# A GELU layer and its gradients on one core: new order of q's rests, one units' slot moved, w1's gradient's rests first, first stores behind a load

## The chip, the core and the metric

The kernel runs on one core of a Trainium2 chip. A core has a matrix engine (TensorE, in the profile PE, its weight loads PEld), VectorE (DVE), ScalarE (ACT), GpSimd (POOL) and SyncE (SP), which here only issues transfers. Each engine works through its own instruction stream in order, and engines wait for one another through semaphores. Matmuls read on-chip memory and write PSUM, eight banks of 512 float32 columns on 128 rows of partitions; VectorE and ScalarE empty those banks. The metric is the device time of one execution in microseconds (us); lower is better.

## The reference: what is computed

A layer with x of 2048 rows and D = 448 columns, a hidden width of F = 1792, in bfloat16, and the gradients of all its inputs for a given grad_out g:

```python
def _fwd_reference(x, w1, b1, w2, b2):
    h = jnp.einsum("bsd,df->bsf", x, w1) + b1
    h = _gelu(h)
    return jnp.einsum("bsf,fd->bsd", h, w2) + b2
...
    _out, _vjp = jax.vjp(_f, x, w1, b1, w2, b2)
    _grads = _vjp(grad_out)
```

So there are six large products: u = x w1, h = gelu(u + b1), out = h w2 + b2; q = g w2 transposed, gh = q times the derivative of gelu at u, the gradient of x = gh w1 transposed; then the gradient of w1 = x transposed times gh, and that of w2 = h transposed times g. The gradients of b1 and b2 are sums of gh and g over the rows.

## The kernel before

**Tiling.** The rows are worked in 4 blocks of 512 columns (`SB`), the hidden width in 14 tiles of 128, two tiles to a step: 28 steps numbered k (or f where u is meant; f runs two steps ahead). u and q of a step are two PSUM banks each, with 512 columns. The contraction over D = 448 is three full tiles of 128 and a rest of 64.

**Row halves.** From the third step on almost every matmul of the first two phases is a half product: it uses 64 of the array's 128 rows, the low or the high ones (`half_product`, L259; the matmul is L265). Half products are emitted in pairs, one low, one high, into two different banks (`side_by_side`, L308), and run beside each other. A bank that was written from one half and is next written from the other needs a turn: L260 to L264 put an empty PE instruction ahead that waits for the last matmul of the old half, unless PE has waited for a later one already. The rests of 64 rows lie in one half only (`u_tail`, `q_tail`): in blocks 0 and 1 u's rest is low and q's high, in blocks 2 and 3 the other way round, so that rests of u and q run beside each other.

**Units.** A unit is 128 rows of out (kind o) or of the gradient of x (kind x): one bank, 14 tiles of contraction in h or gh. Two units are open together and are worked as pairs of half products (`units_side`); `second` True is the other half of the contraction. Units' pairs are put between the groups of u and q to give banks time to turn or to be emptied. A finished unit is evicted (`evict`, L437): VectorE adds b2 for kind o, ScalarE copies for kind x, into one of five staging tiles, and POOL's queue stores it.

**Single steps** (L556 to L622, k = 1 to 11). A step emits u's first group (three pairs), units, u's second group with the banks exchanged between the halves, units, the rests of u and q, units, q's first group, units, q's second group, units; `between` lists the units' pairs of these places. ScalarE copies u out of its banks (`copy_u`, L345), then squares, gelu and tanh; VectorE makes the derivative and the product gh (`dve_gh`, L403), which frees q's banks. In the single steps u's banks are the same two each time.

**Double steps** (L646 to L696, k = 12, 14, ... 26). Two steps at once, the odd k and the even k. `pe_tails` (L284) emits u's rests for the next pair interleaved with q's rests for this one; `pe_q_rows` then emits the groups of q, the odd k first. q of the even k has PSUM tile two0. q of the odd k has PSUM tile two1, which in between holds the two units of the step (`open_two(1, 2)`, L675). These are evicted in the next step inside `dve_gate` (L365), from k = 16 on behind its second scalar addition.

**The last phase.** x and g are loaded once more with rows on partitions, gh has been turned by transposing transfers (`turn_gh`) and h was stored and comes back transposed. The gradient of w1 is made in `gw1_full` (L778; 16 matmuls of 128x128 for each of three tiles of D and four groups of columns) and, for the 64 rest columns of x, in `gw1_tail` (L788): pairs of 128x64 matmuls side by side in the array's column halves. Then come the 14 tiles of w2's gradient (`gw2_tile`, L809). Sums for the biases run on VectorE and POOL beside it.

**Queues.** The order on each engine is the order of emission, written out by hand. SP issues nearly all loads, all transposing transfers and the stores of h; POOL the stores of units and a few copies; ACT the stores of the weights' gradients. `behind` (L125) puts an empty instruction on an engine that waits for a transfer.

Of the kernel before, what the change touches and what calls it, by code (L numbers as in the profile page):

```python
# [19 lines left out]
def kernel(  # L20
# [15 lines left out]
    nc = tc.nc  # L36
    P = 128
# [10 lines left out]
    NPAIR = NF // 2  # L48
    NSTEP = NB * NPAIR
    NSINGLE = 12  # L50
# [4 lines left out]
    WIDE = (0, 1)  # L55
# [27 lines left out]
    w1T_sb = const.tile([P, NF, D], BF16, name="w1T_sb")  # L83
# [41 lines left out]
    def behind(eng, transfer):  # L125
        tc.add_manual_dep(eng.nop().ins, transfer.ins.name, mybir.DependencyInfo(mybir.DependencyClass.Sync, mybir.DependencyReason.DATA),
                          reason="loads behind what is needed first")
# [49 lines left out]
    nc.gpsimd.dma_start(out=b2_bc[:], in_=b2.rearrange("(o d) -> o d", o=1).to_broadcast((P, D)))  # L177
    load_w2T(0, 256)
    def load_w1T(t0, t1):
        nc.sync.dma_start_transpose(out=w1T_sb[:, t0:t1, :], in_=w1[:, t0 * P:t1 * P])  # L180

    load_w1T(2, 8)
    load_w1T(8, 12)
    load_g(1)
    load_w1T(12, NF)
    load_w1T(0, 2)

    pw = two_banks(1, "pw")
    for w in range(NWAKE):
# [57 lines left out]
    def half(up):  # L247
        return slice(DL, P) if up else slice(0, DL)

    def open_q(k):  # L250
        b, p = divmod(k, NPAIR)
        if p == 0:
            ghT[b] = blk.tile([P, NF, SB], BF16, name="ghT", tag="ghT")
        PQ[k] = two_banks(0 if k < NSINGLE else order_b[k % 2], "pq")

    LOW, HIGH = slice(0, DL), slice(DL, P)
# [17 lines left out]
    def q_tail(k, a, swap=False):  # L274
        b, p = divmod(k, NPAIR)
        hf = half((b in WIDE) != swap)
        g = g_swap[b] if swap else gT[b][:, 0, :]
        half_product(("q", k, a), PQ[k][:, a, :], w2T[hf, 0, cols(p, a)], g[hf, :], hf, True, False)
# [5 lines left out]
    def pe_tails(fs, ks):  # L284
        cross = bool(fs) and bool(ks) and (fs[0] // NPAIR in WIDE) != (ks[0] // NPAIR in WIDE)
        for k in ks:
            open_q(k)
        us = [(f, a) for f in fs for a in range(2)]
        qs = [(k, a) for k in ks for a in range(2)]
        if not us and len(ks) == 2:  # L290
            for a in range(2):
                q_tail(ks[0], a)
                q_tail(ks[1], a, swap=True)
            return
        for n in range(max(len(us), len(qs))):
            if n < len(us):
                u_tail(*us[n])
            if n < len(qs):
                q_tail(*qs[n], swap=cross)
# [28 lines left out]
    def units_side(uns, second, tiles=range(NF)):  # L328
        one, other = uns[::-1] if second else uns
        side_by_side(unit_of(one, tiles), unit_of(other, tiles))  # L330
        for un in uns:
            un.slots += len(tiles)
        if one.slots == 2 * NF:
            for un in uns:
                un.done = NPAIR
                open_units.remove(un)
                finished.append(un)
# [139 lines left out]
    def evictions(most=NS):  # L477
        for un in finished[:most]:
            un.evict()
        del finished[:most]  # L480
# [42 lines left out]
    uns = [open_units[0:2], open_units[2:4]]  # L523
# [6 lines left out]
    def two_units(banks):  # L530
        for n in banks:
            open_unit(one_bank(n, "ps")[:, 0:D])
        return open_units[-2:]

    def fill(part):
        if isinstance(part, tuple):
            part = [(part[0], part[1], t) for t in part[2]]
        for uns, second, t in part:
            units_side(uns, second, [t])

    def tiles(p):
        return range(2 * p, 2 * p + 2)
# [12 lines left out]
    act_gelu([2])  # L555
    for i in range(1, NSINGLE):  # L556
        f = i + LEAD
        if i < 6:
            between = [(uns[1], False, tiles(i)), (uns[0], True, tiles(i)[:1]), (uns[0], True, tiles(i)[1:]), (uns[1], True, tiles(i))]
        elif i == 6:  # L560
            between = [(uns[0], True, tiles(i)), (uns[1], False, tiles(i)[:1]), (uns[1], False, tiles(i)[1:]), (uns[1], True, tiles(i))]
        else:
            if i == 7:
                ahead, later = xs, two_units((2, 3))
                slots = [(ahead, False, t) for t in range(6, NF - 2)] + [(later, False, t) for t in range(4)]
                slots += [(ahead, False, t) for t in range(NF - 2, NF)] + [(later, False, t) for t in range(4, NF)]
                slots += [(ahead, True, t) for t in range(NPAIR)] + [(later, True, t) for t in range(NF)]
                slots += [(ahead, True, t) for t in range(NPAIR, NF)]
            between = [slots[2 * c:2 * c + 2] for c in range(5)]
            del slots[0:10]  # L570
        open_u(f)
        open_q(i)
        if i == 1:
            fill(between[0])
        side_by_side(u_of(f, 0, True), u_of(f, 1, True))
        if i > 1:
            fill(between[0])
        else:
            fill(between[1])
        side_by_side(u_of(f, 1), u_of(f, 0))  # L580
        if i > 1:
            fill(between[1])
        pe_tail_pair(f, i, 1)
        pe_tail_pair(f, i, 0)
        fill(between[2])
        side_by_side(q_of(i, 0), q_of(i, 1))
        fill(between[3])
        side_by_side(q_of(i, 1, True), q_of(i, 0, True))
        if i < 6:
            units_side(uns[0], False, tiles(i + 1))  # L590
        elif i > 6:
            fill(between[4])
        if i > 1:
            act_tanh([i])
        if i == 6:
            evictions(2)
        copy_u(f, "aa")
        if i == NSINGLE - 1:
            evictions(2)
        act_square([f])  # L600
        if i == NSINGLE - 1:
            evictions()
        act_gelu([f])
        if i == 1:
            dve_chain("both 1", "cubic 2", "gate 1", "cubic*u 2", "slope 2", "gh 1", "slope*h 2", "cubic 3")
        elif i < NSINGLE - 1:
            dve_chain(f"both {i}", f"cubic*u {i + 1}", f"gate {i}", f"slope {i + 1}", f"gh {i}", f"slope*h {i + 1}", f"cubic {f}")
        else:
            dve_chain(f"both {i}", f"cubic*u {i + 1}", f"gate {i}", f"slope {i + 1}", f"slope*h {i + 1}", f"gh {i}",
                      f"cubic {f}", f"cubic*u {f}", f"slope {f}", f"slope*h {f}")  # L610
        if i == 6:
            evictions()
            open_two(1, 2)
            xs = open_units[-2:]
            units_side(xs, False, range(0, 6))
        if i == 9:
            nc.gpsimd.dma_start(out=g_low[0:DL, :], in_=gT[1][DL:P, 0, :])
            g_swap[1] = g_low
        if i < 8 or i % 2:
            traffic(i if i < 8 else (i + 7) // 2)  # L620
        if i > 6:
            stores(2, f - 1)  # L622
# [23 lines left out]
    for n in range(nq):  # L646
        i = 10 + n
        k = NSINGLE + 2 * n
        ks = [k, k + 1]
# [22 lines left out]
        if nxt:  # L672
# [3 lines left out]
            uns = open_units[-2:]  # L676
# [5 lines left out]
        elif fs:  # L682
            uns, held = two_units(order_a[2:4]), two_units(order_a[0:2])
# [17 lines left out]
    for banks in (order_a[2:4], None, order_a[0:2], order_a[2:4]):  # L701
        if banks is None:
            open_two(0, 2)
            uns = open_units[-2:]
        else:
            uns = two_units(banks)
# [81 lines left out]
    def gw1_tail(ft0, n):  # L788
        ps = bank_w()
        for st_ in range(NS):  # L790
            b, j = PLACE[st_]
            for h in range(2):
                nc.tensor.matmul(ps[h * DL:(h + 1) * DL, 0:n * P], lhsT=x_nat[:, st_, KF * P:D],  # L793
                                 rhs=gh_nat[:, b, ft0 + h * n:ft0 + (h + 1) * n, j, :], start=(st_ == 0), stop=(st_ == NS - 1),
                                 tile_position=(0, h * DL), skip_group_check=True)
        o = stg.tile([P, SB], BF16, name="st", tag="st")
        nc.scalar.copy(out=o[:, 0:n * P], in_=ps[:, 0:n * P])
        for h in range(2):
            t0, t1 = ft0 + h * n, ft0 + (h + 1) * n
            while t0 < t1:  # L800
                t2 = t0 + 1
                while t2 < t1 and f_at(t2) == f_at(t2 - 1) + P:
                    t2 += 1
                c0 = (t0 - ft0 - h * n) * P
                queued.append(nc.scalar.dma_start(out=out_2[KF * P:D, f_at(t0):f_at(t0) + (t2 - t0) * P],
                                                  in_=o[h * DL:(h + 1) * DL, c0:c0 + (t2 - t0) * P]))
                t0 = t2

    def gw2_tile(ft, halves):  # L809
# [8 lines left out]
            queued.append(nc.scalar.dma_start(out=out_4[ft * P:(ft + 1) * P, h * w:(h + 1) * w], in_=o[:, 0:w]))  # L818
        return done

    for ft0, n in ((0, 4), (4, 4), (8, 4), (12, 2)):
        for kt in range(KF):
            gw1_full(ft0, n, kt)
            emit_sum(3)
        if ft0 == 12:
            gw1_tail(0, 4)
            gw1_tail(8, 3)
    for ft in range(NF):
        last = gw2_tile(ft, 2 if ft == NF - 1 else 1)
        if ft + 4 < NF:  # L830
# [35 lines left out]
```

## Time and profile before

| | |
|---|---|
| median of 3 runs (lowest to highest) | 266.71 us (266.71 to 266.94) |
| the profiled execution's own time | 267.09 us |
| its span, first to last instruction | 265.3 us |
| TensorE busy (2171 matmuls) | 261.6 us, 99% |
| VectorE, ScalarE, GpSimd busy | 174.8, 137.4, 42.7 us |
| transfers, mean over the span | 168 GB/s |

How to read it: all engines run at once, so busy times do not add up, and the span is set by the chain of work that ended last. A matmul's recorded duration overlaps the next one's, because matmuls are pipelined; what one costs on a busy engine is the distance from its start to the next start of the same half. A row of the timeline gives start, length, engine, line, operation, written tile <- read tiles, shapes, and xN for N merged instructions; in brackets how long the engine had been idle and what released it. Rows with SPq, ACTq or POOL and DMA are issues of transfers; the time to landing is in the list of DMA issues. In the windows a row is a stretch (us from the span's start), its length, the busy time of the engine with its number of instructions, TensorE's granted clock as a share of full speed, the share of the transfer engines in use and GB/s.

The phases in the span: wake-up matmuls and full-array products up to about 12 us, single steps to 68 us, double steps to 153 us, the last units to 177 us, w1's gradient to 220 us, w2's gradient to 263 us.

### The profile page before, as it was taken

How to read it: one execution, taken by the hardware profiler on the slowest of the kernel's cores; microseconds unless marked ns; L12 is line 12 of the kernel's file. 1: busy time of each engine (PE TensorE's matmuls, PEld its weight loads, DVE VectorE, ACT ScalarE, POOL GpSimd, SP SyncE). 2: the span in 40 equal slices, each digit the busy share in tenths (PEclk: the TensorE clock that was granted, in tenths of full speed). 3: DMA queues.
4: the chain of work that ended last, by engine and by line, in shares of the span. 5: the costliest groups of instructions: out<-in, count | busy, mean ns of one | idle time of the engine just before them, and what ended most of it. 6: DMA issues, size and time to landing. Idle time of an engine off the chain costs nothing.

```text
span 265.3 us, 5207 instructions
## 1 busy us (share of the span) xinstructions
PE 261.6 (99%) x2171; PEld 148.9 (56%) x2171; DVE 174.8 (66%) x217; ACT 137.4 (52%) x164; POOL 42.7 (16%) x54
## 2 busy tenths in 40 slices
PE   8999999999999999999999999999999999999995
PEld 3444444444466565555658888864444765555554
DVE  1599999999998978769897731129999991000000
ACT  2799997887997686877749410022111111121111
POOL 1003003300302021010311111220700008900000
PEclk9999999999999999999999999999999999999999
DMA  7999999999999999465381359999211102999851
GB/s 177 234 239 197 215 216 153 227 101 259 282 220 193 248 206 268 89 171 110 95 161 49 67 125 308 349 164 276 81 40 40 49 22 56 212 216 224 203 129 35
DMA packets 111511, 44.47 MB, mean 168 GB/s; under 512 B 91104, under 2 KB 110272, under 8 KB 111488
## 3 DMA queue, kind: packets, MB, share of 16 engines
q1 hardware_dynamic: 104256, 35.79, 65.3%
q0 software_dynamic: 1984, 4.65, 7.2%
q10 hardware_dynamic: 5248, 3.71, 4.7%
q8 instruction: 17, 0.28, 0.4%
q14 instruction: 6, 0.05, 0.1%
HBM read 7.23 MB, written 14.23 MB: 81 GB/s over the span
## 4 chain that ended last, share of the span: by engine, by line
PE 99%; ACT 0%; issue 0%
PE ps L265 32%; PE ps_v L814 16%; PE pu L265 16%; PE pq L265 15%; PE ps_w L782 14%; PE ps_w L793 2%; PE pw L190 2%; PE pu L244 2%; PE pu L505 0%; PE ps L431 0%; ACT st L817 0%
## 5 line engine op out<-in xcount | busy, mean ns | idle before, releaser
L265 PE MATMUL pq<-gT,w2T 64*128 64x512 bf16 x386 | 55.6, 376 | 0.0
L265 PE MATMUL ps<-w_sb,hT 64*128 64x448 bf16 x440 | 49.0, 349 | 0.0
L265 PE MATMUL ps<-w1T_sb,ghT 64*128 64x448 bf16 x448 | 48.8, 349 | 0.0
L345 ACT ACTIVATE U<-pu,b1T 128x512 bf16<-128x512 f32 x54 | 33.5, 688 | 18.9 <-PE pu L265 14.4
L814 PE MATMUL ps_v<-g_nat,h_nat 128*128 128x448 bf16 (+1 forms) x240 | 42.6, 340 | 0.0
L403 DVE SCALAR_TENSOR_TENSOR ghT<-AZ,pq 128x1024 bf16<-128x1024 bf16 x28 | 33.9, 1218 | 12.3 <-PE pq L265 11.8
L265 PE MATMUL pu<-xT,w_f 64*128 64x512 bf16 x300 | 41.4, 376 | 0.0
L444 POOL DMA_DIRECT2D out_dram<-st x32 | 19.8, 625 | 133.3 <-DVE st L443 70.9
L265 PEld LDWEIGHTS <-ghT 64*128 64x128 bf16 x448 | 28.9, 94 | 15.3
L782 PE MATMUL ps_w<-gh_nat,x_nat 128*128 128x512 bf16 (+1 forms) x192 | 36.5, 352 | 0.0
L265 PEld LDWEIGHTS <-hT 64*128 64x128 bf16 x440 | 26.4, 94 | 17.0 <-issue 0.5
L265 PEld LDWEIGHTS <-w2T 64*128 64x128 bf16 x392 | 26.4, 94 | 14.9 <-PE pq L265 1.0
L814 PEld LDWEIGHTS <-h_nat 128*128 128x128 bf16 x240 | 23.3, 98 | 19.3 <-DMA out_dram<-st 0.3
L363 ACT ACTIVATE AZ<-AZ 128x1024 bf16<-128x1024 bf16 (+1 forms) x20 | 27.8, 1391 | 6.8 <-DVE AZ L359 6.8
L768 DVE TENSOR_TENSOR acc<-acc,gh_nat 128x1792 f32<-128x1792 f32 x14 | 30.0, 2142 | 0.5
L782 PEld LDWEIGHTS <-x_nat 128*128 128x128 bf16 x192 | 18.7, 98 | 17.9 <-issue 0.4
L354 ACT ACTIVATE AZ<-U 128x1024 bf16<-128x1024 bf16 (+1 forms) x21 | 28.2, 1342 | 0.9 <-DVE U L347 0.4
L351 ACT ACTIVATE hT<-U 128x1024 bf16<-128x1024 bf16 (+1 forms) x22 | 28.0, 1277 | 0.0
L817 ACT CAST st<-ps_v 128x448 bf16<-128x448 f32 (+1 forms) x15 | 7.6, 507 | 34.8 <-PE ps_v L814 34.8
L265 PEld LDWEIGHTS <-w_f 64*128 64x128 bf16 x300 | 16.2, 94 | 15.0 <-issue 0.7
L441 ACT CAST st<-ps 128x448 bf16<-128x448 f32 x16 | 7.8, 539 | 29.3 <-PE ps L265 27.6
L785 ACT CAST st<-ps_w 128x512 bf16<-128x512 f32 (+1 forms) x12 | 6.4, 532 | 27.7 <-PE ps_w L782 27.7
(58 smaller groups left out, 192.2 us busy)
## 6 DMA issues: line engine op xcount, KB each, us to landing
hT_dram<-hT SPq DMA_DIRECT2D x28, 256.0 KB, 3.2
out_dram<-st POOLq DMA_DIRECT2D x32, 112.0 KB, 4.7
x_nat<-in_x_dram SPq DMA_DIRECT2D x1, 1792.0 KB, 10.2
g_nat<-in_grad_out_dram SPq DMA_DIRECT2D x1, 1792.0 KB, 15.6
out_dram<-st ACTq DMA_DIRECT2D x13, 112.0 KB, 3.3
out_dram<-st ACTq DMA_DIRECT2D x9, 128.0 KB, 1.7
w_f<-in_w_dram SPq DMA_DIRECT2D x5, 192.0 KB, 3.8
w_sb<-in_w_dram SPq DMA_DIRECT2D x3, 224.0 KB, 3.8
```

What stands on the lines that cost most here:

```text
L265: mm = nc.tensor.matmul(ps, lhsT=w, rhs=m, start=start, stop=stop, tile_position=(hf.start, 0), skip_group_check=True)
L345: nc.scalar.activation(out=dst, in_=PU[f][a][:], func=ACT.Identity, bias=bias)
L351: nc.scalar.activation(out=rows(hT, r), in_=part_u(r), func=ACT.Gelu_apprx_tanh)
L354: nc.scalar.activation(out=part_a(ks), in_=part_u(ks), func=ACT.Square, scale=math.sqrt(3.0 * GELU_A * GELU_C))
L363: nc.scalar.activation(out=z, in_=z, func=ACT.Tanh, scale=-1.0 / 3.0)
L403: nc.vector.scalar_tensor_tensor(out=rows(ghT, [k]), in0=part_z([k]), scalar=1.0, in1=PQ[k][:], op0=ALU.subtract if single else ALU.add, o ...
L441: nc.scalar.copy(out=st[:, 0:D], in_=self.ps)
L444: pooled.append(nc.gpsimd.dma_start(out=(out2 if self.kind == "o" else gx2)[r:r + P, :], in_=st[:, 0:D]))
L768: last_sum[:] = [nc.vector.tensor_tensor(out=v, in0=in0, in1=gh_nat[:, b, :, j, :], op=ALU.add)]
L782: nc.tensor.matmul(ps[:, 0:n * P], lhsT=x_nat[:, st_, kt * P:(kt + 1) * P], rhs=gh_nat[:, b, ft0:ft0 + n, j, :], start=(st_ == 0), stop=(s ...
L814: nc.tensor.matmul(ps[:, 0:w], lhsT=h_nat[ft][:, st_, :], rhs=g_nat[:, st_, h * w:(h + 1) * w], start=(st_ == 0), stop=(st_ == NS - 1))
L817: done = nc.scalar.copy(out=o[:, 0:w], in_=ps[:, 0:w])
```

## The change

Four edits, with no change of any product, shape or type.

1. In `pe_tails`, where there are rests of u and both k of a double step are above 13 (k = 14 to 24), q's rests no longer come as odd bank 0, odd bank 1, even bank 0, even bank 1. They come as even bank 0, an odd bank, the other odd bank, even bank 1; bank 1 is the first of the odd ones where q's rests lie in the low half, which is so for all these steps.
2. In the first single step (i = 1) one pair of units' half products moves from between u's two groups to ahead of u's first group (the fourth u, f = 3), and the pairs behind move up by one: between q's two groups stands one pair where there were two.
3. `gw1_tail(0, 4)` and `gw1_tail(8, 3)` are emitted ahead of the twelve `gw1_full`, not behind them.
4. In single step 6, ahead of the first evictions, POOL's queue waits for the last load of w1 transposed (`load_w1T(0, 2)`), which is why `load_w1T` now returns its transfer.

```diff
     def load_w1T(t0, t1):
-        nc.sync.dma_start_transpose(out=w1T_sb[:, t0:t1, :], in_=w1[:, t0 * P:t1 * P])
+        return nc.sync.dma_start_transpose(out=w1T_sb[:, t0:t1, :], in_=w1[:, t0 * P:t1 * P])
...
-    load_w1T(0, 2)
+    last_tiles = load_w1T(0, 2)
...
         qs = [(k, a) for k in ks for a in range(2)]
+        if us and len(ks) == 2 and ks[0] > NSINGLE + 1:
+            odd, even = ks
+            low = half((odd // NPAIR in WIDE) != cross) == LOW
+            qs = [(even, 0), (odd, 1 if low else 0), (odd, 0 if low else 1), (even, 1)]
...
-        if i < 6:
+        if i == 1:
+            between = [(uns[0], True, tiles(1)[1:]), None, (uns[1], True, tiles(1)[:1]), (uns[1], True, tiles(1)[1:])]
+        elif i < 6:
             between = [(uns[1], False, tiles(i)), (uns[0], True, tiles(i)[:1]), (uns[0], True, tiles(i)[1:]), (uns[1], True, tiles(i))]
...
         if i == 1:
-            fill(between[0])
+            units_side(uns[1], False, tiles(1))
+            units_side(uns[0], True, tiles(1)[:1])
         side_by_side(u_of(f, 0, True), u_of(f, 1, True))
-        if i > 1:
-            fill(between[0])
-        else:
-            fill(between[1])
+        fill(between[0])
         side_by_side(u_of(f, 1), u_of(f, 0))
...
         if i == 6:
+            behind(nc.gpsimd, last_tiles)
             evictions(2)
...
+    gw1_tail(0, 4)
+    gw1_tail(8, 3)
     for ft0, n in ((0, 4), (4, 4), (8, 4), (12, 2)):
         for kt in range(KF):
             gw1_full(ft0, n, kt)
             emit_sum(3)
-        if ft0 == 12:
-            gw1_tail(0, 4)
-            gw1_tail(8, 3)
```

## The prediction

> **What bounds the kernel now.** I read the page's busy shares first, then the chain that ended last, then the length of each double step by windows, and only then the timeline at the places that the change touches.
>
> ```profile
> span 265.3 us, 5207 instructions
> PE 261.6 (99%) x2171; PEld 148.9 (56%) x2171; DVE 174.8 (66%) x217; ACT 137.4 (52%) x164; POOL 42.7 (16%) x54
> ...
> PE 99%; ACT 0%; issue 0%
> ```
>
> PE is the whole chain, so an edit counts only by what it does to the spacing of matmul starts. Busy time cannot show that: a matmul's modelled duration (376 ns for 512 columns) covers the next start. The double steps are alike, so I compared their lengths from one point of the units to the same point a step later, for the steps with k = 14, 16, 18, 20 and, from another equal pair of points, 22 (columns: stretch, its length, PE busy, clock, DMA).
>
> ```profile
> 78.91:90.36 11.45, 11.45 (x115) 1.00 1.15 235
> 90.36:101.82 11.46, 11.46 (x115) 1.00 1.00 210
> 101.82:113.16 11.34, 11.34 (x115) 1.00 0.73 163
> 113.16:124.50 11.34, 11.34 (x115) 1.00 0.46 119
> 121.21:132.67 11.46, 11.46 (x114) 1.00 0.47 119
> ```
>
> Equal work at an equal clock takes 11.34 us in two steps and 0.11 to 0.12 more in three. The timeline at the rests of the second, third and last of the reordered steps says why.
>
> ```profile
> 92.08 1.16 DVE L443 TENSOR_TENSOR st<-ps,b_bc 128x448 bf16<-128x448 f32 x2
> ...
> 93.16 0.38 PE L265 MATMUL pu<-xT,wt 64*128 64x512 bf16 x1
> 93.29 0.37 PE L265 MATMUL pq<-gT,w2T 64*128 64x512 bf16 x1
> 93.37 0.38 PE L265 MATMUL pu<-xT,wt 64*128 64x512 bf16 x1
> ...
> 104.62 0.38 PE L265 MATMUL pq<-gT,w2T 64*128 64x512 bf16 x1
> ...
> 138.75 0.38 PE L265 MATMUL pu<-xT,wt 64*128 64x512 bf16 x1
> 138.88 0.37 PE L265 MATMUL pq<-gT,w2T 64*128 64x512 bf16 x1
> ...
> 84.84 2.52 DVE L403 SCALAR_TENSOR_TENSOR ghT<-AZ,pq 128x1024 bf16<-128x1024 bf16 x2 [0.59 <-PE pq L265]
> ```
>
> The two 64-row halves run as two streams, each with a start every 0.216 us (93.16 to 93.37 for u's rests in the high half). The first rest of q, that of the odd k, should start beside u's at 93.16 and starts at 93.29: its bank held the two units of the step before, and the second of their VectorE evictions ends at 92.08 + 1.16 = 93.24. That stream lags by 0.13 and the step pays for it when the streams meet again. In the steps at 101.82 and 113.16 the units are of the x kind, ScalarE evicts them earlier, and q's first rest starts at 104.62, on time.
>
> **The change part by part.**
>
> *q's order.* It applies where the step has u's rests and k is 14 to 24: six steps. All their rests of q use the low half, so the order becomes even bank 0, odd bank 1, odd bank 0, even bank 1. The even bank's last reader is the second of the two products at 84.84, done at 84.84 + 2.52 = 87.36, 5.8 us before 93.16, so the first rest no longer waits. The odd tile is now met one slot later, at 93.37, after its release at 93.29: 0.08 to spare. Count, operands and halves of the matmuls stay, and so does the number of turns (a turn is PE's wait before a bank is written from the other half): odd bank 1 was second before and is second after, and the other rests are as far from their turn or on the half that follows. Gain: 0.11, 0.12 and 0.12 from the windows (k = 14, 16, 22), nothing for 18 and 20, and for k = 24, which has no like step behind it, the lag itself, 138.88 - 138.75 = 0.13, which nothing afterwards shows taken back. Sum 0.48. Low end: nothing, if the release comes a slot later too; high end 0.50. A loss is excluded by the even bank's 5.8 us and by the odd bank's later slot, unless the evictions themselves move.
>
> *The slot ahead of the fourth u.* Here are the first single step on PE, and ScalarE's copies of the third u, which free the two banks of the fourth.
>
> ```profile
> 14.13 1.25 ACT L345 ACTIVATE U<-pu,b1T 128x512 bf16<-128x512 f32 x2
> 18.11 1.26 ACT L345 ACTIVATE U<-pu,b1T 128x512 bf16<-128x512 f32 x2
> ...
> 14.28 0.93 PE L265 MATMUL ps<-w_sb,hT 64*128 64x448 bf16 x8
> 15.05 1.19 PE L265 MATMUL pu<-xT,w_f 64*128 64x512 bf16 x6
> 15.88 0.55 PE L265 MATMUL ps<-w_sb,hT 64*128 64x448 bf16 x2
> 16.29 0.82 PE L265 MATMUL pu<-xT,w_f 64*128 64x512 bf16 x6
> ...
> 17.59 0.81 PE L265 MATMUL pq<-gT,w2T 64*128 64x512 bf16 x6
> 18.24 0.54 PE L265 MATMUL ps<-w_sb,hT 64*128 64x448 bf16 x4
> 18.62 0.81 PE L265 MATMUL pq<-gT,w2T 64*128 64x512 bf16 x6
> 19.27 0.35 PE L265 MATMUL ps<-w_sb,hT 64*128 64x448 bf16 x2
> ```
>
> u's first three pairs open at 15.05, but the copies end at 14.13 + 1.25 = 15.38, and the high half starts behind them. These pairs and the one units pair behind them therefore take 1.24 us up to 16.29, where 3 x 0.216 + 0.19 = 0.84 would do (the row at 18.24 has two units pairs in 18.62 - 18.24 = 0.38, so 0.19 each). The change puts one units pair into that hole: u opens in the low half at 15.24, and the high half still waits for the copy. So u's last pair and the turn behind it, at 16.29, do not move; one pair is still between them. What moves is the pair that is missing later: between q's two groups stood two units pairs (18.24), now stands one, and q's second group could start at 18.62 - 0.19 = 18.43. But its turn waits for the last matmul of the first group. That one starts at about 17.59 + 2 x 0.216 = 18.02 and ends at 17.59 + 0.81 = 18.40; from the like turn at 16.29 (u's group of 15.05 ends at 15.05 + 1.19 = 16.24) some 0.05 to 0.06 is the signal, so the second group starts at about 18.46 and its second pair may lose 0.01 more. Gain: 18.62 - 18.47 = 0.15, at most the whole pair, 0.19, at least nothing. The next thing in line is ScalarE's next copies, done at 18.11 + 1.26 = 19.37: the following u starts two units pairs after 19.27, at 19.65 before and at 19.50 after, and with 0.05 for the signal (as from 93.24 to 93.29 above) 0.08 is left. I take 0.14.
>
> *w1's gradient's rests first.* The same 64 matmuls, two copies and five stores move from behind the twelve full groups to ahead of them. The matmuls cost the same there. What differs is how often the array's shape changes.
>
> ```profile
> 211.81 1.91 PE L782 MATMUL ps_w<-gh_nat,x_nat 128*128 128x256 bf16 x16
> 213.65 0.62 PE L793 MATMUL ps_w<-gh_nat,x_nat 128*64 128x512 bf16 x4
> ...
> 219.08 0.82 PE L793 MATMUL ps_w<-gh_nat,x_nat 128*64 128x384 bf16 x8
> 219.83 0.74 PE L814 MATMUL ps_v<-g_nat,h_nat 128*128 128x448 bf16 x3
> ...
> L793 PE MATMUL ps_w<-gh_nat,x_nat x64: 326/352/403, 213.7 to 219.6; 128*64 128x512 bf16 x32, 128*64 128x384 bf16 x32
> L782 PE MATMUL ps_w<-gh_nat,x_nat x192: 272/379/389, 177.2 to 213.4; 128*128 128x512 bf16 x144, 128*128 128x256 bf16 x48
> ```
>
> Sixteen 256-column matmuls take 1.91 us and the last lasts 0.272, so they are (1.91 - 0.272) / 15 = 0.109 apart, the last starts at 213.45, and the next start was due at 213.56: it is 213.65, 0.09 lost on entering 128x64. Likewise four pairs of 0.82 us with a last one of 0.326 are 0.165 apart, the next start was due at 219.73, and it is 219.83: 0.10 lost on leaving. Before, the shape goes 64x128, 128x128, 128x64, 128x128: three changes. After, 64x128, 128x64, 128x128: two, and the step from w1's to w2's gradient keeps its shape. I take 0.10 for the one saved. No row shows 64x128 straight to 128x64: if it costs nothing extra the gain could be 0.2, if it costs two of the known changes the gain is nothing, and at three it is a loss of 0.1. The Trainium skill (TensorEngine Tiling, Key Properties) says that a change of tiling mode, not of the tile alone, drains the engine; by it the direct step is one drain like the others, and the trace agrees with a drain's 0.09 and 0.10 at the two places that it shows.
>
> Does the moved work find its data? x_nat below is issued at 158.82 and lands in 10.2 us, 169.0, and the last turn of gh_nat is issued ahead of it on the same queue; the rests start at 177.2. Their copies and stores go to a half-idle ScalarE (52%), and no bank is met again before a group of at least 2.5 us has passed. The sums on VectorE and the loads of h_nat for w2's gradient keep their order on their queues.
>
> *First stores behind the last of w1T.*
>
> ```profile
> 38.12 2.63 SPq L180 DMA_TRANSPOSE w1T_sb<-in_w_dram  x2
> 40.62 1.49 POOL L444 DMA_DIRECT2D out_dram<-st  x2 [15.00 <-DVE st L443]
> w1T_sb<-in_w_dram SPq DMA_TRANSPOSE x2, 4.0
> xT<-in_x_dram SPq DMA_TRANSPOSE x2, 11.6
> 67.64 0.60 PE L265 MATMUL pu<-xT,w_f 64*128 64x512 bf16 x4
> 158.82 0.44 SPq L716 DMA_DIRECT2D x_nat<-in_x_dram  x1
> x_nat<-in_x_dram SPq DMA_DIRECT2D x1, 1792.0 KB, 10.2
> ```
>
> The second of the two loads is issued near 39.5 and lands near 43.5 to 44, so POOL's wait holds two stores by some 3 us. Behind them on POOL stand the next two stores, the copies of the other halves and a copy of g, none needed before the double steps (67.64); four of the five staging tiles are in use, so no eviction waits. Cost to PE: nothing; a faster last transpose is worth nothing either, since no PE row waits for it. Both ends lie with what a late transfer can do (the third rival).
>
> Sum: 0.48 + 0.14 + 0.10 = 0.72 us. The profiled execution took 267.09 us with a span of 265.3; it should become about 264.6 of span and 266.4. The median of the runs shown is 266.71, 0.38 below the profiled one, and 266.71 - 0.72 = 265.99.
>
> **The rivals.** *The wait only moves* (q's order gives nothing): odd bank 1 has 0.08 us in hand, and VectorE is nearly unbroken from 84.84 to the evictions. If these end 0.13 later against PE, the same lag arises at the second slot. Against it: that run of VectorE begins at a wait for PE (0.59 at 84.84), so it shifts with PE. Then 0.24 remain: 266.47, no change that can be told.
>
> *The small terms fail*: if one of the slot and the shape change gives nothing, 266.09 to 266.13, still faster; if neither does, 266.23.
>
> *Slower, by a late transfer*: two stores pushed from 40.6 to 44 now fall among the transposes that follow. The third block of x (the two xT transfers above) takes 11.6 us already and lands near 60; PE needs it at 67.64. It decides once the block lands over 7.5 us later, and beyond that each microsecond is one of PE: at 10 us later 266.71 - 0.72 + 2.5 = 268.5. Against it: the same bytes move in the same stretch, only 3 us later. The Trainium skill (DMA: Bandwidth & Descriptors, Issuing engines are not separate DMA queues) says that transfers of all queues interleave on the same 16 engines, which is the way by which POOL's stores could delay SP's transposes.
>
> **How the numbers follow.** About 0.2% (0.53 us) is what a measurement of this kernel can tell from no change. Forecast 0.55 (265.99, own range 265.8 to 266.15); one small term missing 0.15; the wait moves 0.12; both small terms missing 0.08; a late transfer or something unseen 0.10. So faster 0.70, same 0.20, slower 0.10. All high ends together give 0.50 + 0.19 + 0.2 = 0.89, 265.8, and runs differ by 0.2, so the range starts at 265.6; it ends at 266.55, above the case of the moved wait, and leaves out the slower ones.
>
> **What would show it.** q's order right: all double steps 11.34 long, q's first rest beside u's. The slot right: q's second group of the first single step at 18.46, the next u at 19.50. The rests right: one jump of 0.1 less, and no gap ahead of w2's gradient. The held stores right: no PE start later than before between 40 and 70. It is wrong if a wait for VectorE appears at the second rest, if the first change of shape costs over 0.2, or if PE waits for a transfer.

## The result and the profile after

The changed kernel takes 266.37 us (median of 16 runs, 265.98 to 266.65) where the kernel before takes 266.88 us (16 runs beside it). The ratio is 0.9977 with a 95% interval of 0.9967 to 0.9986: 0.6 us less, between 0.4 and 0.9. The difference is small, 0.23%, and clear of the runs' noise. The profiled execution's span fell from 265.3 to 264.6 us. From the page after:

```profile
span 264.6 us, 5203 instructions
PE 260.9 (99%) x2171; PEld 130.8 (49%) x2171; DVE 174.7 (66%) x217; ACT 137.4 (52%) x164; POOL 42.0 (16%) x54
...
PE 99%; ACT 0%; issue 0%
```

PE is still the whole chain, and busy shares say nothing: 99% before and after. The windows of the double steps k = 14 to 20 and 22, cut at the same instructions as those of before, say where 0.46 us went (columns: stretch, length, PE busy, clock, DMA).

```profile
78.74:90.08 11.34, 11.34 (x115) 1.00 1.02 218
90.08:101.42 11.34, 11.34 (x115) 1.00 1.08 236
101.42:112.76 11.34, 11.34 (x115) 1.00 0.78 174
112.76:124.10 11.34, 11.34 (x115) 1.00 0.45 118
120.82:132.16 11.34, 11.34 (x114) 1.00 0.48 120
```

All five are 11.34 us, where three had 11.45 or 11.46. The timeline at the rests of k = 16, VectorE's row first:

```profile
91.79 1.16 DVE L447 TENSOR_TENSOR st<-ps,b_bc 128x448 bf16<-128x448 f32 x2
...
92.88 0.38 PE L265 MATMUL pq<-gT,w2T 64*128 64x512 bf16 x1
92.89 0.38 PE L265 MATMUL pu<-xT,wt 64*128 64x512 bf16 x1
93.10 0.38 PE L265 MATMUL pq<-gT,w2T 64*128 64x512 bf16 x1
93.10 0.38 PE L265 MATMUL pu<-xT,wt 64*128 64x512 bf16 x1
```

The first rest of q starts beside u's, at 92.88. The evictions end at 91.79 + 1.16 = 92.95, and the odd bank's rest at 93.10 finds its tile free.

The first single step and its copies by ScalarE:

```profile
14.09 1.25 ACT L349 ACTIVATE U<-pu,b1T 128x512 bf16<-128x512 f32 x2
...
14.29 1.11 PE L265 MATMUL ps<-w_sb,hT 64*128 64x448 bf16 x10
15.23 0.96 PE L265 MATMUL pu<-xT,w_f 64*128 64x512 bf16 x6
...
16.26 0.82 PE L265 MATMUL pu<-xT,w_f 64*128 64x512 bf16 x6
...
17.56 0.81 PE L265 MATMUL pq<-gT,w2T 64*128 64x512 bf16 x6
18.21 0.35 PE L265 MATMUL ps<-w_sb,hT 64*128 64x448 bf16 x2
18.44 0.82 PE L265 MATMUL pq<-gT,w2T 64*128 64x512 bf16 x6
```

u's second group (16.26) stands where it stood against ScalarE's copies, which are 0.04 earlier in this execution; q's second group starts 18.44 - 16.26 = 2.18 after it, where it was 18.62 - 16.29 = 2.33.

The last phase, at the changes of the array's shape:

```profile
175.93 0.73 PE L265 MATMUL ps<-w1T_sb,ghT 64*128 64x448 bf16 x6
176.59 0.41 PE L798 MATMUL ps_w<-gh_nat,x_nat 128*64 128x512 bf16 x2
...
182.02 0.82 PE L798 MATMUL ps_w<-gh_nat,x_nat 128*64 128x384 bf16 x8
182.77 0.61 PE L787 MATMUL ps_w<-gh_nat,x_nat 128*128 128x512 bf16 x2
...
218.44 0.82 PE L787 MATMUL ps_w<-gh_nat,x_nat 128*128 128x256 bf16 x6
219.10 0.54 PE L819 MATMUL ps_v<-g_nat,h_nat 128*128 128x448 bf16 x2
```

The row at 175.93 ends at 176.66; its last matmul lasts 0.35, as the pair at 18.21 does, so it started at 176.31, the next start was due 0.19 later, at 176.50, and came at 176.59: 0.09. Leaving the column halves costs about 0.09 again (last start 182.84 - 0.326 = 182.51, next due 0.165 later). Into w2's gradient: last start 219.26 - 0.272 = 218.99, due 0.109 later, 219.10, and it is 219.10: nothing.

### The profile page after: what moved, and what is told of

Its sections match the earlier page's. It is cut to its first block, busy times and chain, and to the rows that moved or that the text cites. A ratio compares the mean times of both kernels' runs of the same rounds, so it can differ in the third digit from the quotient of the medians.

```text
span 264.6 us, 5203 instructions
## 1 busy us (share of the span) xinstructions
PE 260.9 (99%) x2171; PEld 130.8 (49%) x2171; DVE 174.7 (66%) x217; ACT 137.4 (52%) x164; POOL 42.0 (16%) x54
## 4 chain that ended last, share of the span: by engine, by line
PE 99%; ACT 0%; issue 0%
PE ps L265 32%; PE pq L265 16%; PE ps_v L819 16%; PE pu L265 14%; PE ps_w L787 14%; PE ps_w L798 2%; PE pw L190 2%; PE pu L244 2%; PE pu L509 0%; PE ps L435 0%; ACT st L822 0%
## 5 line engine op out<-in xcount | busy, mean ns | idle before, releaser
L265 PE MATMUL ps<-w1T_sb,ghT 64*128 64x448 bf16 x448 | 48.1, 349 | 0.0
L448 POOL DMA_DIRECT2D out_dram<-st x32 | 19.1, 602 | 133.9 <-DVE st L447 71.5
L265 PE MATMUL pu<-xT,w_f 64*128 64x512 bf16 x300 | 40.3, 376 | 0.0
L265 PEld LDWEIGHTS <-ghT 64*128 64x128 bf16 x448 | 21.9, 94 | 22.3
L265 PEld LDWEIGHTS <-hT 64*128 64x128 bf16 x440 | 22.5, 94 | 20.7 <-issue 0.5
L265 PEld LDWEIGHTS <-w2T 64*128 64x128 bf16 x392 | 21.4, 94 | 22.5 <-PE pq L265 1.3
L265 PEld LDWEIGHTS <-w_f 64*128 64x128 bf16 x300 | 14.6, 94 | 16.2 <-issue 0.5
```

The costliest lines, as they stand in the source:

```text
L265: mm = nc.tensor.matmul(ps, lhsT=w, rhs=m, start=start, stop=stop, tile_position=(hf.start, 0), skip_group_check=True)
L448: pooled.append(nc.gpsimd.dma_start(out=(out2 if self.kind == "o" else gx2)[r:r + P, :], in_=st[:, 0:D]))
```

## The experiments

All ratios are against the kernel before on the same chip.

**1. Each edit alone.** From the kernel before, the diff of one edit only: q's order (`e1_order`), the slot (`e2_slot`), the rests first (`e3_rests`), the hold (`e4_hold`).

> The kernel before with the new order of q's rests alone. Theory (the odd bank is released by its units' eviction 0.13 us after the first slot): all five compared double steps 11.34 us long, q's first rest beside u's in all six, span 265.32 - 0.46 to 0.48 = 264.85, time 0.17 to 0.18% below the kernel before. Rival (the wait only moves to the second slot, or the length comes from the turns): steps of 11.45 remain, span 265.3.

> The kernel before with the moved units' slot of the first single step alone. Theory: q's second group of that step at 18.45 to 18.47 instead of 18.62, the next u 0.14 to 0.15 earlier, every later start up to 150 us earlier by the same, the double steps as long as before; span 265.17, time 0.05% lower, hard to tell by times alone. Rival (the following copies of ScalarE or VectorE's products take it back): the next u at 19.65 again, or a new wait before 45 us, span 265.3.

> The kernel before with the rests of w1's gradient first, alone. Theory (one change of the array's shape fewer, each some 0.1): the first gap, from row halves to column halves, 0.09 to 0.10, the gap from the column halves to the full array 0.10, no gap on entering w2's gradient; span 265.22, time 0.04% lower. Rival (a direct change from row halves to column halves costs two drains, or the start of w2's gradient still waits): span 265.3 or above.

> The kernel before with the held first stores alone. Theory: nothing; the first stores leave at about 44 us instead of 40.6, no start of TensorE moves by over 0.02, span 265.3. Rival (a late transfer): the third block of x lands later than 60 us and, if later than 67.6, TensorE stalls there; each microsecond beyond is one of time.

| edit alone | ratio (95% interval) | by PE's starts in its profile |
|---|---|---|
| q's order | 0.9981 (0.9973 to 0.9989) | all double steps 11.34; -0.46 us from their first to the last units |
| slot | 0.9996 (0.9985 to 1.0006) | see below; double steps as before |
| rests first | 0.9992 (0.9981 to 1.0003) | 176.91 to 219.42 for w1's gradient, 42.51 where it was 177.23 to 219.83, 42.60; w2's gradient behind it 0.01 shorter |
| hold | 0.9990 (0.9973 to 1.0007) | stores leave at 43.90 instead of 40.62; from 6 us on every start of PE 0.03 to 0.05 later than before, and none against another |

q's order is the change: alone it has most of the ratio of all four. Its window of k = 14 and, for contrast, the same one of the slot alone:

```profile
78.40:89.74 11.34, 11.34 (x115) 1.00 1.09 225
```

```profile
78.37:89.82 11.45, 11.45 (x115) 1.00 1.13 223
```

The slot did neither what the theory nor what the rival expected. These are the first single step without the slot (q's order alone) and with it (the slot alone):

```profile
14.15 0.92 PE L265 MATMUL ps<-w_sb,hT 64*128 64x448 bf16 x8
14.90 0.81 PE L265 MATMUL pu<-xT,w_f 64*128 64x512 bf16 x6
...
15.78 0.82 PE L265 MATMUL pu<-xT,w_f 64*128 64x512 bf16 x6
...
19.14 0.38 PE L265 MATMUL pu<-xT,w_f 64*128 64x512 bf16 x2
```

```profile
14.07 1.11 PE L265 MATMUL ps<-w_sb,hT 64*128 64x448 bf16 x10
15.01 0.81 PE L265 MATMUL pu<-xT,w_f 64*128 64x512 bf16 x6
...
19.10 0.38 PE L265 MATMUL pu<-xT,w_f 64*128 64x512 bf16 x2
```

In both, u's first group takes 0.81 us, unhindered: in these executions ScalarE's copies are not late. From the units to the next u it is 19.14 - 14.15 = 4.99 without the slot and 19.10 - 14.07 = 5.03 with it, so here the slot costs 0.04 to 0.05, a second turn with one pair in front of it. Before and after, where the copies are late, it was 19.65 - 14.28 = 5.37 and, from 14.29, 5.19. What differs is the execution, not only the kernel: in some, PE waits ahead of the step for a load, as in this row of `e12_two` of experiment 5, a kernel without slot and hold,

```profile
12.30 0.39 PE L265 MATMUL pq<-gT,w2T 64*128 64x512 bf16 x1 [0.18 <-DMA w2T<-in_w_dram]
```

and ScalarE, which does not wait for it, then has its copies ready in time. So the slot is worth from -0.05 to +0.18, and its ratio cannot be told from 1. One profile of each kernel gives an idea of the mean (all but `e9_two`, which moves a second pair): the five kernels without the slot take 4.98 to 5.37 over this stretch, 5.17 on the mean, the eight with it 5.03 to 5.23, 5.11 on the mean.

**2. Release or turn.** From the changed kernel, q's rests with the odd banks last:

```diff
-            qs = [(even, 0), (odd, 1 if low else 0), (odd, 0 if low else 1), (even, 1)]
+            qs = [(even, 0), (even, 1), (odd, 0 if low else 1), (odd, 1 if low else 0)]
```

> The changed kernel with q's rests in the order even bank 0, even bank 1, odd bank 0, odd bank 1. The odd bank's release is then early by 0.3 us, but odd bank 1's rest stands last, right ahead of the group that writes this bank from the high half. Theory (the place of odd bank 1 is set by its turn: last start + 0.376 + 0.06): in all six steps the high half of q's first group starts some 0.2 us late, each step 0.15 to 0.2 longer, span 264.57 + 0.9 to 1.2 = 265.5 to 265.8. Rival (only the release matters, a turn this near is free): steps 11.34, span 264.6.

The ratio is 1.0038 (1.0023 to 1.0053), slower than before. One of its five windows, which are all of the same length:

```profile
78.89:90.50 11.61, 11.61 (x115) 1.00 1.10 239
```

Every step is 0.27 longer, those whose units ScalarE evicts too, so it is not the release: odd bank 1's rest right ahead of the group that writes the bank from the other half makes PE wait for its end. The direction was expected, the size not (0.15 to 0.2 a step): in k = 16 that rest ends at 93.92 + 0.38 = 94.30 and the high half starts at 94.43, 0.13 behind it where 0.06 was reckoned; why, stays open. This shows why the odd tile has to come later than first, but its bank 1 not last.

**3. The release moved.** From the changed kernel, the evictions one VectorE instruction later:

```diff
-        if between is not None:
-            between()
         nc.vector.tensor_scalar(out=z_, in0=z_, scalar1=1.0, scalar2=None, op0=ALU.add)
+        if between is not None:
+            between()
```

> The changed kernel with the evictions inside the gate placed one VectorE instruction (0.69 us) later in the steps k = 16, 22 and 24 whose units VectorE evicts; k = 14 evicts at another place and keeps it, in k = 18 and 20 ScalarE evicts. Theory (the second eviction's end releases the odd tile, with 0.10 us in hand): q's second rest starts about 0.55 to 0.6 late in these three steps and they are that much longer, k = 18 and 20 stay at 11.34; span 266.1 to 266.4. Rival (the release is not what the rests wait for): steps 11.34, span 264.6.

The ratio is 1.0025 (1.0015 to 1.0035). k = 16, VectorE and PE, and the windows of k = 16 and 18:

```profile
92.36 1.15 DVE L447 TENSOR_TENSOR st<-ps,b_bc 128x448 bf16<-128x448 f32 x2
...
92.94 0.38 PE L265 MATMUL pq<-gT,w2T 64*128 64x512 bf16 x1
92.94 0.59 PE L265 MATMUL pu<-xT,wt 64*128 64x512 bf16 x2
93.57 0.37 PE L265 MATMUL pq<-gT,w2T 64*128 64x512 bf16 x1
93.57 0.39 PE L265 MATMUL pu<-xT,wt 64*128 64x512 bf16 x1
```

```profile
90.13:101.88 11.75, 11.71 (x115) 1.00 1.08 216
101.88:113.22 11.34, 11.34 (x115) 1.00 0.66 141
```

The evictions end at 92.36 + 1.15 = 93.51 and q's second rest starts at 93.57, 0.06 behind. The step is 0.41 longer, and only the steps whose units VectorE evicts are. That the rests wait for the evictions is shown. The size was taken too large: an instruction of 0.69 moved the evictions by about 0.5 against PE (from 92.95 - 93.10 = -0.15 to 93.51 - 93.16 = 0.35), because neighbouring instructions overlap on VectorE: the moved one starts 0.61 behind the scalar addition ahead of it and the evictions 0.60 behind the moved one (91.15, 91.76, 92.36), where without it they start 0.70 behind that addition (91.09, 91.79).

**4. The shape changes.** From the changed kernel, `gw1_tail(8, 3)` back behind the full groups:

```diff
     gw1_tail(0, 4)
-    gw1_tail(8, 3)
     for ft0, n in ((0, 4), (4, 4), (8, 4), (12, 2)):
...
+        if ft0 == 12:
+            gw1_tail(8, 3)
```

> The changed kernel with the second rest of w1's gradient put back behind the full groups: the array's shape then changes four times, not twice. Theory: two more drains of 0.09 to 0.10, span 264.57 + 0.2 = 264.75 to 264.8; all starts up to 180 us unchanged. Rival (the gain came from the data or the stores of the last phase, not from the shape): span within 0.05 of 264.57 or of the kernel before's last phase, 264.67.

```profile
176.85 0.84 PE L798 MATMUL ps_w<-gh_nat,x_nat 128*64 128x512 bf16 x6
...
217.69 1.96 PE L798 MATMUL ps_w<-gh_nat,x_nat 128*64 128x384 bf16 x22
219.58 0.93 PE L819 MATMUL ps_v<-g_nat,h_nat 128*128 128x448 bf16 x4
```

w1's gradient takes 219.58 - 176.85 = 42.73 us, against 219.10 - 176.59 = 42.51 with two changes and 42.60 with three: 0.09 to 0.12 for each. The ratio is 0.9988 (0.9978 to 0.9997). The span of this execution, 265.1, is not comparable beyond that: other parts of it, among them a wait of 0.07 near 45 us, differ from the changed kernel's.

**5. What the slot and the hold are worth.** Four more kernels. `e9_two` moves the pair that stands between u's two groups ahead as well:

> The changed kernel with the second units' pair of the first single step, too, ahead of the fourth u, so that none stands between u's two groups. Theory (the hole ahead of u is filled by one pair already; ScalarE's copy ends at 15.39 and u's second group waits for its turn): u opens in both halves at about 15.43, its second group at about 16.29 against 16.26, the next u 0 to 0.03 later than in the changed kernel, span 264.57 to 264.60. Rival (every units' pair moved ahead is worth 0.15): the next u at 19.33, span 264.4.

Its copies were not late, so the hole that it was to test was not there. u's second group started 0.23 late in both halves, since no pair hid the turn in front of it, and the next u came 5.23 behind the units, 0.20 later than with the slot and copies in time (5.03). In that state a second pair ahead loses; for the other it remains untested. Its ratio is 0.9974 (0.9965 to 0.9983), not to be told from the changed kernel's.

`e12_two` has q's order and the rests first, without slot and hold:

> The new order of q's rests and the rests of w1's gradient first, without the moved slot and without the hold. Theory: 0.46 + 0.105 = 0.57 us below the kernel before in the stretches behind 20 us, time ratio about 0.9979; the two edits left out are together worth within 0.1 us in times, because whether ScalarE's copies are late for the fourth u differs from execution to execution. Rival (slot and hold are worth 0.14 and more in every execution): ratio 0.9984 where the whole change has 0.9977 or less.

All stretches behind 20 us are as expected: double steps of 11.34, 42.51 for w1's gradient. The ratio, 0.9990 (0.9975 to 1.0006), is too wide to decide between the two, since one run was at 268.45; the median is 266.15 where that of before on the chip is 266.77, a ratio of 0.9977 like that of the whole change, which speaks for the theory without showing it.

`e10_late` and `e11_late_free` make the last loads of w1 transposed late, with and without the hold, by reading parts of w1 once more ahead of them into space that is written later. The diff is that of both; `e11_late_free` also leaves out the hold's line, `behind(nc.gpsimd, last_tiles)`:

```diff
+    for t0, t1 in ((2, 8), (8, 12)):
+        nc.sync.dma_start_transpose(out=gh_nat[:, 3, t0:t1, :, :].rearrange("p ft j f -> p ft (j f)")[:, :, 0:D], in_=w1[:, t0 * P:t1 * P])
     load_w1T(12, NF)
```

> The changed kernel with two extra transposing loads (a second reading of w1 into space of gh_nat that is written later) ahead of the last two loads of w1 transposed, so that these are issued some 4.5 us later, near 43 to 44, and land near 46 to 48. TensorE wants the first of them at about 45.4 and should wait for it, 0.5 to 2 us. With the held stores in place. Theory (holding the stores is worth nothing to a transposing load): TensorE's wait equal within 0.2 to that of the like kernel without the hold.

> The same late loads without POOL's wait: the first stores leave at about 40.6 and 45.9. Theory: the last two loads of w1 transposed land within 0.3 of the kernel with the held stores, the wait of TensorE near 45 us equal within 0.2. Rival (the hold is there to shield the last loads from the stores): they land 0.5 us or more later than with the hold, and TensorE waits that much longer.

The issue of the first of the two late loads with its time to landing, and PE's row behind it, with the hold:

```profile
43.17 3.52 SPq L180 DMA_TRANSPOSE w1T_sb<-in_w_dram  x2
w1T_sb<-in_w_dram SPq DMA_TRANSPOSE x1, 4.9
48.08 0.93 PE L267 MATMUL ps<-w1T_sb,ghT 64*128 64x448 bf16 x4 [2.49 <-DMA w1T_sb<-in_w_dram]
```

and without:

```profile
42.06 4.77 SPq L180 DMA_TRANSPOSE w1T_sb<-in_w_dram  x2
w1T_sb<-in_w_dram SPq DMA_TRANSPOSE x1, 6.1
48.23 0.55 PE L267 MATMUL ps<-w1T_sb,ghT 64*128 64x448 bf16 x4 [3.06 <-DMA w1T_sb<-in_w_dram]
```

In this pair the load took 6.1 instead of 4.9 us without the hold. But it was issued 1.1 us earlier and landed only 0.15 later (48.19 against 48.04; the second load 50.01 against 49.55), and 0.42 of the 0.57 us by which PE waited longer are that PE came to the row 0.42 earlier (its last starts ahead of the wait are at 44.80 and at 45.22). For the first load the theory holds (within 0.3), for the second it does not, and neither comes to the rival's 0.5.

That the stores lengthened the load is not shown either. In the kernels without extra loads the second of the two loads runs beside the first stores when these are not held: it took 4.1 to 4.9 us there (five kernels without the hold) and 4.1 to 5.8 with it (seven kernels). The first took up to 6.3 us with the hold, in `e7_split`, where the first store left after it had landed.

The ratios, 1.0115 (1.0067 to 1.0163) with and 1.0125 (1.0104 to 1.0145) without the hold, do not part the two, since PE's clock fell in some executions of both (the last section). At a mean granted clock of 1.000 there are two executions of each, 268.58 and 268.80 with the hold, 269.65 and 269.71 without: a hint that here it was worth 1 us. A part of that is in the profile of `e11_late_free` and is not at the loads: at k = 14 ScalarE had waited 1.71 us for a store of h, the evictions came late, ended at 83.83 + 1.15 = 84.98, and q's second rest started behind them at 85.03, which cost 0.42. The hold's worth beside a late load thus stays open.

Without the extra loads PE waited 0.07, 0.25 and 0.44 us for the first of the two loads in `e7_split`, `e9_two` and the kernel of experiment 6, all with the hold. SP issued it there at 39.3 to 40.9 instead of 38.1 as before, ahead of any store. What makes it late in those executions was not settled.

**6. One gap more.** In the first double step the second half of the units starts 0.1 late behind its turn, before and after. `e8_first` puts a pair of u more in front of it and lets the odd banks of k = 14 come third and fourth, since the units end one pair later:

```diff
+            more = 0 if n else 1
+            side_by_side(u_of(nxt[1], 1), u_of(nxt[1], 0), slice(0, more))
             units_side(uns, True)
-            side_by_side(u_of(nxt[1], 1), u_of(nxt[1], 0))
+            side_by_side(u_of(nxt[1], 1), u_of(nxt[1], 0), slice(more, None))
...
+            if odd == NSINGLE + 3:
+                qs = [(even, 0), (even, 1), (odd, 1 if low else 0), (odd, 0 if low else 1)]
```

> The changed kernel with one pair of u more between the two halves of the units in the first double step, where the high half of the units starts 0.10 us late behind its turn, and with q's rests in the order even 0, even 1, odd 1, odd 0 in the step behind it (k = 14), since its units then end one pair nearer to the rests. Theory: that gap gone, the rests of k = 14 without a wait for VectorE, the turn of odd bank 1 from the third place at most 0.02 late; the stretch from the first double step's units to the last units 0.08 to 0.11 shorter than in the changed kernel, span 0.1 lower. Rival (the units' eviction takes it back): q's odd rest in k = 14 late by 0.1, no gain.

```profile
77.81 0.68 PE L265 MATMUL pu<-xT,w_f 64*128 64x512 bf16 x4
78.24 1.11 PE L265 MATMUL ps<-w_sb,hT 64*128 64x448 bf16 x9
...
81.97 0.38 PE L265 MATMUL pq<-gT,w2T 64*128 64x512 bf16 x1
82.06 0.38 PE L265 MATMUL pu<-xT,wt 64*128 64x512 bf16 x1
```

The gap is gone (two pairs from 77.81, the units at 78.24, 0.43 = 2 x 0.216 later) and nothing is won: the two halves come out of it 0.09 apart and are still so at the rests (81.97 and 82.06), and from the first matmul of these units to the last one of the last units it is 176.87 - 75.16 = 101.71 us, where the changed kernel has 176.31 - 74.63 = 101.68. The halves are already apart ahead of the gap (a wait of the high half for ScalarE's copies at 74.3 in the changed kernel); the gap was the place where that was paid. The ratio is 0.9984 (0.9974 to 0.9995). No kernel here beats the changed one by more than the runs can tell.

## Why the prediction was right

It gave 0.72 us less; the times gave 0.6 (0.4 to 0.9), the spans 0.75. The median of 266.37 lies in the whole range, 265.6 to 266.55, but 0.38 above the forecast of 265.99 and outside the forecast's own range, 265.8 to 266.15. Of the 0.38, 0.17 is that the kernel before had a median of 266.88 in the runs beside it and not 266.71. Reckoned from 266.88 the forecast would be 266.16, and the time lies nearer to the case with both small terms missing, 266.40; the interval holds both. What shows the small terms is the starts of PE, not the time. That the spans agree to 0.03 is in part luck: the slot's share is there because both profiled executions had late copies by ScalarE. By its steps:

- *q's order, 0.48*: 0.46 by starts, of which k = 24 has 0.12 where 0.13 was taken. The even bank was free, the odd tile met one slot later with time in hand (0.08 predicted, 0.10 found: 93.10 against 92.95 + 0.05 = 93.00), turns as before. Experiments 1 and 3 show the cause, experiment 2 that the turn binds only when odd bank 1 stands last.
- *The rival that the wait only moves*: it did not, because the evictions shifted with PE, 91.79 and 92.08 while the first rest went from 93.16 (u's) to 92.88. It comes true when the evictions are half a microsecond later (experiment 3, and of itself in the profile of `e11_late_free`).
- *The slot, 0.14*: right for the profiled pair, 2.33 to 2.18, and so was 18.46 for q's second group (18.44). Wrong as a term of every run. The step that failed is that ScalarE's copies hold back the fourth u: one execution showed it, and others show them in time. There the slot costs 0.05. The trace of before could not have told: in the five profiles without the slot the next u starts anywhere between 19.14 and 19.69. From a single execution the term needed a range down to a small loss.
- *The rests first, 0.10*: 0.10. The direct change from row halves to column halves cost 0.09, like the others; experiment 4 adds two changes and 0.22 us. The Trainium skill's rule (TensorEngine Tiling, Key Properties: a change of tiling mode drains the engine) holds at all places that these traces show, and the one that no row of before showed came out by it.
- *The hold, nothing*: no start of PE moved against another with the hold alone, nor between 36 and 75 us in the profiled pair. The step that failed is its reason, "a faster last transpose is worth nothing either, since no PE row waits for it": that is true of the one execution shown, where the load landed 3.8 us ahead of its row (41.79, 45.56), and in three others PE waited 0.07 to 0.44 us for it. Whether holding the stores makes that load faster is not shown (experiment 5).
- *The late transfer*: the third block of x never stopped PE. What did in some executions was the first of the last two loads of w1 transposed, of which the prediction said that no PE row waits for it. The Trainium skill (DMA: Bandwidth & Descriptors, Issuing engines are not separate DMA queues) says that transfers of all queues interleave on the same engines. The first transposing transfer of gh, issued behind these loads, agrees in direction: without extra loads it took 9.4 to 14.0 us in the five kernels without the hold and 8.3 to 10.4 in the seven with it. The next one, issued at 53 to 59, took 6.7 to 11.9 without the hold and 7.8 to 13.8 with it, so no saving over both is seen, and that the stores are the cause is not shown.

## What to carry to other kernels

On an engine that is busy all along, compare repeated steps of equal work: a step that is longer than its twin names the place, and the wait is then found by one release time against one start. Where two streams share an engine, a gap is often not made where it stands; look for the earlier place where one stream fell behind. A gain in the first microseconds, or a margin to a load, needs more than one execution before it is counted.

## What the runs showed of the hardware

- The two row halves keep a lag between them: with one of them late by 0.13 us, the other goes on at its spacing of 0.216 us, and the lag is carried unchanged over whole phases. The kernel before carried 0.13 us from 138.9 to the end of the units at 177; it is paid where both must stand together. A wait that outlasts one spacing stops both halves: in experiment 3 q's second rest waits until 93.57, and u's third rest, due in the other half at 93.37, starts at 93.57 too.
- After a wait of 2.5 us PE ran at about half its clock for some 3 us in the profiled execution of `e10_late`, and after one of 3.1 us in that of `e11_late_free` it did not. First the stretch behind the wait in `e10_late`, then in `e11_late_free` (columns: stretch, length, PE busy, clock, DMA):

```profile
48.00:51.20 3.20, 3.12 (x18) 0.53 1.34 211
```

```profile
48.20:51.20 3.00, 2.96 (x30) 1.00 1.26 245
```

  The shorter wait was the dearer one: 18 matmuls in 3.2 us against 30 in 3.0. It is a matter of the execution, not of the kernel: two of the four executions of `e10_late` have a mean clock of 0.994 (270.51 and 272.17 us), two have 1.000 (268.58 and 268.80), and `e11_late_free` has two at 1.000 as well. The Trainium skill (TensorE: Matmul & The Clock Gate, Part 1: The HAM clock gate) says that the clock is set by activity in a free-running window of about 3.4 us, which fits a drop in some executions only. It also puts the low clock behind at least one idle window, and the 2.5 us here are shorter than one: there the measurement decides.
